# Gated mix of sliding attention and a gated MLP on one core: the last stage's loads, one subtraction, the exponentials and the V weights placed otherwise

## The chip, the cores and the metric

The kernel runs on one core of a Trainium2 chip. The metric is the device time of one execution in microseconds (us). Engines are named as in the profile: PE (matrix), PEld (its weight loads), DVE (vector), ACT (scalar), POOL and SP (here mostly queues that issue DMAs). Each engine works through its own instructions in the order in which the program lists them, and semaphores make it wait for the others.

## The reference

```python
x = A_x                                            # 1 x 2048 x 1024, bf16
g = sigmoid((x * gate_w).sum(-1, keepdims=True))
# A: attention, 32 heads of 32; each position sees itself and 7 earlier ones, 2 apart
q, k, v = heads(x @ wqkv)
logits = einsum("bhsd,bhswd->bhsw", q, k[window]) * 32 ** -0.5   # masked before the start
a = (softmax(logits) weighted sum of v[window]) @ wo
# B: gated MLP, 1024 -> 3584 -> 1024
h = gelu(x @ w_gate) * (x @ w_up)
b = h @ w_down
out = g * a + (1 - g) * b
```

## The kernel before

All matrix products are done by Strassen-like schemes with seven products in place of eight, so DVE has many additions and subtractions of operands and results beside PE's products.

**Units.** The first part is a row of 78 units (0 to 77). Each multiplies 256 weight columns by half of the positions (1024, "s" = 0 or 1): units 0 and 1 are a gate/up pair, 2 to 17 are Q and K, 18 to 25 are V, 26 to 77 are gate (even) and up (odd) units. A unit has seven products, each of four matmuls 128x512 (all at line 362): p1, p5, p26 (two), p73 (two), p4. In step b of the main loop PE gets p1(b), p73(b-1), p5(b), p26(b), p4(b-1), so 28 matmuls. ACT copies a product X to Y's bank after p1 (line 380), puts p5's product aside (385), evacuates X after p26 (368 with Gelu in gate units, 370 otherwise), copies Y to bank Z (392), and evacuates Y after p4. DVE adds p5's part to both Y and Z after p73 (line 399, one instruction for a unit, called "the L399 of unit u" here). p4(u) writes to the bank that the L399 of unit u reads, and ACT's copy to Z (392) of unit u+1 overwrites the other one, so both come after it.

**Background tasks.** All else that DVE does is cut into tasks: generators that issue one instruction or so and yield its estimated cost. `run_bg` is called at the end of each step with a budget of about 4.8 us, and lets the awake task of the lowest priority number go on until the budget is spent. So a task's instructions stand behind the L399 of unit b-1 and ahead of that of unit b. `due` finishes a task at the beginning of a step, `at` puts a call there, `at_end` at the end of one.

Tasks that matter here:
- `qk_prods` (594) and `spill` (594, 645) multiply Q and K; the sums over the head dimension are matmuls (599). The last block of each half is the "spill", done from DRAM copies.
- `softmax` subtracts the maximum (683, 685), `softmax_exp` issues the exponential on ACT (691), which needs another table than Gelu, `softmax_back` sums and normalises (699, 701, 702, 704) and stores the weights.
- `sums_v` (542) makes sums of the V weights, which `load_v` loads; `sums_pair` (319) does so for the gate/up weights.
- `t_forms` (851) makes four combinations of the weights of the last stage (w_down and wo stacked, "R") into DRAM (t_d), with loads at line 837 and three buffers; it stops when V's weights need that memory (`tf_close`, at the end of step TFE-1 = 14), and reloads its buffers when the V units are done.
- `pv_all` multiplies attention weights and V (740, 747) and stores the result o (767).

**Last stage.** `down(s)` multiplies [h, o] by R, once for each half s, with products of 72 matmuls 128x512 (line 1031, `mm`) and, one level further, of 126 matmuls 128x256 (line 1006, `level2`). A quarter Aij has 18 rows of blocks: 0 to 11 and 12, 13 are h, 14 to 17 are o. `mm` takes them in the order 0 to 11, 14 to 17, 12, 13. For s = 0, h must first be multiplied by 1-g (`scale_task`, 895). Then `down(0)` is:

- PE: A11 R11, then A12 R21 on top (both 1031), then `level2` of S and T1, then `level2` of S2 and T2, and so on.
- DVE: scales A12, A22 and A21 (nine instructions, three each), S = A21 + A22 and AD = A11 - A21 (`comb_task`, 902, five instructions each), the forms for S and T1 (967 and 975, eight), S2 = A22 - AD (902), `forms_L` of S2 (967, four), A12 - S2 (902, five), `forms_R` of T2 (975, four).

`level2` begins with two products of plain quarters; the third needs the first results of `forms_L` and `forms_R`. The loads of the first half are issued on SP in this order: A12's h rows, A12's o rows, A22's h, A22's o (all in `pre_down_2`, called at the end of `pv_all`), A21's h, A21's o, then the rows 11 to 17 of R21, from w_down and wo, whose first 11 rows are there earlier (`pre_down_3`, at step 77), then T1 and T2. h loads are line 806, o loads 808, R loads 824, T loads 827. The h rows 12 and 13 are loaded on POOL's queue.

Of the kernel before, what the change touches and what calls it, by code (L numbers as in the profile page):

```python
# [9 lines left out]
ALU = mybir.AluOpType  # L10
# [57 lines left out]
def kernel(  # L68
# [64 lines left out]
    with tc.manual_schedule(engines={mybir.EngineType.PE, mybir.EngineType.DVE, mybir.EngineType.Activation,  # L133
# [296 lines left out]
        def bg(gen, prio, wake):  # L430
            t = Task(gen, prio, wake)
            tasks.append(t)
            tasks.sort(key=lambda t_: t_.prio)
            return t
# [2 lines left out]

        def run_bg(b, period):
            credit[0] = min(credit[0], 0.3) + period
            while credit[0] > 0:  # L440
                t = next((t_ for t_ in tasks if t_.wake <= b), None)
                if t is None:
                    break
                c = t.step()
                if c is None:
                    t.wake = b + 1
                else:
                    credit[0] -= c
# [222 lines left out]
        def softmax(a, cnt, b0, e):  # L671
            ee = regf(R_EX[e], cnt * SC)
            e4 = ee.rearrange("p (a w s) -> p a w s", a=cnt, w=NWIN)
            sw = ee.rearrange("p (a w s) -> p a s w", a=cnt, w=NWIN)
            lg = banks[:, b0:b0 + cnt, :]
            src = lg.rearrange("p a (w s) -> p a w s", w=NWIN)
            bc = lambda t_: t_.rearrange("p a (o s) -> p a o s", o=1).to_broadcast([P, cnt, NWIN, SJ])
            if a == 0:
                TT(out=src[:, 0], in0=src[:, 0], in1=mask, op=ALU.add)
                yield 0.6  # L680
            m = md[:, (0, 2, 0, 3, 0)[e]:(0, 2, 0, 3, 0)[e] + cnt, :]
            assert e < 2 or ready >= {2: {0, 1, 2}, 3: {0, 1, 2}, 4: {4, 5, 6}}[e]
            V.tensor_reduce(out=m, in_=lg.rearrange("p a (w s) -> p a s w", w=NWIN), axis=AX.X, op=ALU.max)
            yield 0.55 * cnt + 0.05
            TT(out=e4, in0=src, in1=bc(m), op=ALU.subtract)
            yield 0.55 * cnt + 0.05
            front.add(a)
            bg(softmax_exp(a, cnt, ee, e4, sw, m, bc), 0, now[0] + 1)

        def softmax_exp(a, cnt, ee, e4, sw, m, bc):  # L690
            nc.scalar.activation(out=ee, in_=ee, func=ACT.Exp, scale=scale)
            bg(softmax_back(a, cnt, ee, e4, sw, m, bc), 3, now[0] + 1)
            yield 0.0

        def softmax_back(a, cnt, ee, e4, sw, m, bc):
            while a // BPS not in gated:
                yield None
            d = m
            V.tensor_reduce(out=d, in_=sw, axis=AX.X, op=ALU.add)
            yield 0.9 * cnt + 0.05  # L700
            V.reciprocal(out=d, in_=d)
            TT(out=d, in0=d, in1=gblk[:, a:a + cnt, :], op=ALU.mult)
            yield 0.65 * cnt
            TT(out=attn_all[:, a:a + cnt, :].rearrange("p a (w s) -> p a w s", w=NWIN), in0=e4, in1=bc(d), op=ALU.mult)
            yield 0.55 * cnt + 0.05
            for j in range(NJ):
                nc.gpsimd.dma_start(out=w_d[a:a + cnt, :, j, :].rearrange("a h n -> h a n"),
                                    in_=attn_all[32 * j:32 * j + 32, a:a + cnt, :])
            ready.update(range(a, a + cnt))
            if a == 2 * BPS - 1:  # L710
                two[0] = True
# [74 lines left out]
        at_slot(Q0 + 6, lambda: gate_chunk(2, bank(1)))  # L786
        at_slot(Q0 + 8, lambda: (gate_chunk(3, bank(1)), bg(gate_task(1), 0, Q0 + 8)))
        due(Q0 + NT + 1, bg(late_form3(), 1, Q0 + 8))
        TFE = Q0 + 13
        due(Q0 + 2 * NT, bg(sums_v(), 2, TFE + 2))  # L790
        for s in range(2):
            for t in range(NT):
# [10 lines left out]

        def load_A(b, s, half, c, i0, i1, with_o, eng=nc.sync):
            t0 = s * SUP + c * SC
            eng.dma_start(out=b[:, i0:i1, :], in_=h_src(half, t0, i0, i1))
            if with_o:
                nc.sync.dma_start(out=b[:, NH_:NK, :], in_=o_d[:, half * 4:half * 4 + 4, t0:t0 + SC])

        def h_src(half, t0, i0, i1):  # L810
            return h_d[:, :, t0:t0 + SC].rearrange("p (i two) s -> p i two s", two=2)[:, i0:i1, half, :]
# [10 lines left out]
        def load_R(b, half, nh, i0=0, i1=NK):  # L822
            for sl, src in r_parts(half, nh, i0, i1):
                nc.sync.dma_start(out=b[:, sl, :], in_=src)
# [8 lines left out]
        def tf_load(q):  # L833
            i0 = NP * q
            for k, a in enumerate(((0, 0), (0, 1), (1, 0), (1, 1))):
                for sl, src in r_parts(*a, i0, i0 + NP):
                    nc.sync.dma_start(out=tf[q % 3][k][:, sl.start - i0:sl.stop - i0, :], in_=src)

        def t_forms():
            q = 0  # L840
            while q < NQ:
                if now[0] == TFE - 1 and tf_open[0]:
                    tf_open[0] = False
                    while now[0] < NQKV + 1:
                        yield None
                    for q_ in range(q, min(q + 3, NQ)):
                        tf_load(q_)
                    yield None
                r11, r12, r21, r22 = tf[q % 3]
                for o_, a, b_ in ((r11, r12, r11), (r12, r22, r12), (r22, r22, r11), (r21, r21, r22)):  # L850
                    TT(out=flat(o_), in0=flat(a), in1=flat(b_), op=ALU.subtract)
                    yield 0.71
                for k, t in enumerate((r11, r22, r12, r21)):
                    nc.gpsimd.dma_start(out=t_d[k][:, NP * q:NP * q + NP, :], in_=t)
                if q + 3 < NQ:
                    tf_load(q + 3)
                q += 1
# [29 lines left out]
        def Bs(s):  # L887
            return {k: bufs[v] for k, v in plan[s].items()}

        def scale_task(b, s, c, ia, ib):  # L890
            t0 = s * SUP + c * SC
            om = omgrep[:, t0:t0 + SC].rearrange("p (o s) -> p o s", o=1)
            for i0 in range(ia, ib, 4):
                i1 = min(i0 + 4, ib)
                TT(out=b[:, i0:i1, :], in0=b[:, i0:i1, :], in1=om.to_broadcast([P, i1 - i0, SC]), op=ALU.mult)
                yield 0.05 + 0.273 * (i1 - i0)

        def comb_task(o_, a, b, op, step=4):
            for i0 in range(0, NK, step):
                i1 = min(NK, i0 + step)  # L900
                f = lambda t_: flat(t_[:, i0:i1, :])
                TT(out=f(o_), in0=f(a), in1=f(b), op=op)  # L902
                yield 0.05 + 0.273 * (i1 - i0)
# [21 lines left out]

        KX = int(R_P5A[0] - R_BUF[6])

        def pre_down_2(s):
            B = Bs(s)
            for k, c in (("A12", 0), ("A22", 1)):  # L930
                load_A(B[k], s, 1, c, 0, NE_, True)
                bg(scale_task(B[k], s, c, 0, NE_), 3, n)

        def pre_down_3(s):
            B = Bs(s)
            load_A(B["A21"], s, 0, 1, 0, NE_, True)
            load_R(B["R21"], 1, 0, KX, NK)

        def pre_down_4(s):
            B = Bs(s)  # L940
# [29 lines left out]
        def forms_R(f, b):  # L970
            f = quads(f)
            q = lambda kh, h: quarter(b, kh, h)
            for o_, a, b_, op in ((f[:, 0], q(0, 1), q(0, 0), ALU.subtract), (f[:, 1], q(1, 1), f[:, 0], ALU.subtract),
                                  (q(0, 1), q(1, 1), q(0, 1), ALU.subtract), (f[:, 2], q(1, 0), f[:, 1], ALU.subtract)):
                TT(out=o_, in0=a, in1=b_, op=op)  # L975
                yield 1.3
# [45 lines left out]
        def down(s):  # L1022
# [53 lines left out]
            run(comb_task(A21, A22, AD, ALU.subtract))  # L1076
            S2 = A21
            level2(VT, S, B["T1"], B["L5"], B["R5"])
            rest = [forms_R(B["R6"], B["T2"]), comb_task(A12, A12, S2, ALU.subtract)]
            run(forms_L(B["L6"], S2), *(rest if last else rest[::-1]))  # L1080

            def mid6():
                joins(VT, B["R5"])
# [58 lines left out]
        for b in range(n):  # L1142
            now[0] = b
            for fn in hooks.pop(b, []):
                fn()
            cur = units[b]
            prv = units[b - 1] if b > 0 else None
            cur.p1()
            if prv:
                prv.p73()  # L1150
            cur.p5()
            extra = 0.0
            if slotq:
                slotq.pop(0)()
                extra += 1.6 if b <= QE + 3 else 0.8
            for fn in pre.pop(b, []):
                fn()
                extra += 0.6
            cur.p26()
            if prv:  # L1160
                prv.p4()
            for fn in post.pop(b, []):
                fn()
            run_bg(b, 4.8 + extra)
# [32 lines left out]
```

## Time and profile before

| | us |
|---|---|
| median of 3 runs | 741.98 (740.92 to 743.15) |
| the profiled execution | 740.5 |
| its span | 738.7 |
| PE busy in the span | 721.3 |
| DVE busy in the span | 654.9 |
| ACT busy | 317.3 |
| mean granted clock of PE | 0.993 |

The span goes from the first to the last instruction; the execution's own time is 1.8 us longer. A line of the waits names the waiting engine and line, what ended the waits, their sum in us, their number and the longest. A line of the timeline has start and length in us, engine, line, operation, output and input, shapes, count, and in brackets the engine's idle time before it and what ended that.

### The profile page before, as it was taken

The page shows a single profiled execution, that of the slowest core. Times are in us where ns is not written, and L with a number is a line of the kernel's source. Part 1 is how long each engine was busy: PE and PEld are TensorE (multiplying, and loading weights), DVE is VectorE, ACT ScalarE, POOL GpSimd, SP SyncE. Part 2 cuts the span into 40 slices and gives each one's busy share as a digit, 9 for nine tenths or more (in the row PEclk, how much of TensorE's full clock was granted, in tenths as well). Part 3 has the DMA queues.
Part 4 walks back from the last instruction along what each step waited for, and adds up shares of the span by engine and source line. Part 5 has one row for each costly group of instructions (what it writes and reads, how often), then busy time and mean ns, then how long its engine had stood idle before and what let it go on. Part 6 is the DMA issues. An engine that isn't in the chain of part 4 may idle for free. (4 is left out here: it accounts for less than half of the span.)

```text
span 738.7 us, 10397 instructions
## 1 busy us (share of the span) xinstructions
PE 721.3 (98%) x3945; PEld 394.5 (53%) x3945; DVE 654.9 (89%) x702; ACT 317.3 (43%) x570; POOL 119.6 (16%) x212
## 2 busy tenths in 40 slices
PE   8999999999999999999999999999989899999998
PEld 4466565655544444444444444444438656758573
DVE  3699999979999999999999999997599699799944
ACT  4554445444566655555555555555102211232210
POOL 1224445311201320000010010101100011110001
PEclk9999999999999999999999999999989999999999
DMA  9977864771326964453364836534982875975501
GB/s 279 272 175 233 277 204 133 256 223 72 107 86 179 362 215 147 118 169 108 123 201 119 269 126 210 168 116 153 356 331 94 333 251 185 367 302 177 216 23 58
DMA packets 118882, 143.93 MB, mean 195 GB/s; under 512 B 18944, under 2 KB 102048, under 8 KB 117808
## 3 DMA queue, kind: packets, MB, share of 16 engines
q1 hardware_dynamic: 104624, 101.53, 43.2%
q0 software_dynamic: 13920, 41.21, 16.5%
q8 instruction: 31, 0.51, 0.3%
q10 hardware_dynamic: 288, 0.52, 0.2%
q14 instruction: 19, 0.16, 0.1%
HBM read 101.16 MB, written 39.99 MB: 191 GB/s over the span
## 5 line engine op out<-in xcount | busy, mean ns | idle before, releaser
L362 PE MATMUL banks<-arena 128*128 128x512 bf16 x2184 | 475.4, 379 | 4.2 <-DVE arena L399 2.4
L362 PEld LDWEIGHTS <-arena 128*128 128x128 bf16 x2184 | 240.5, 111 | 238.5 <-issue 10.5
L1031 PE MATMUL banks<-arena 128*128 128x512 bf16 x504 | 113.1, 386 | 4.6 <-DMA arena<-in_B_w_down_dram 3.1
L399 DVE TENSOR_TENSOR arena<-banks,arena 128x1024 bf16<-128x1024 f32 x78 | 95.2, 1220 | 18.9 <-PE banks L362 11.7
L1006 PE MATMUL banks<-arena 128*128 128x256 bf16 x882 | 99.1, 275 | 3.0 <-DVE arena L975 3.0
L385 ACT COPY arena<-banks 128x512 f32<-128x512 f32 x78 | 45.7, 586 | 130.9 <-PE banks L362 130.9
L1006 PEld LDWEIGHTS <-arena 128*128 128x128 bf16 x882 | 87.1, 99 | 15.3 <-issue 3.5
L1031 PEld LDWEIGHTS <-arena 128*128 128x128 bf16 x504 | 50.0, 99 | 65.7 <-issue 9.2
L370 ACT CAST arena<-banks 128x512 bf16<-128x512 f32 x102 | 59.7, 585 | 43.8 <-PE banks L362 43.8
L740 DVE TENSOR_TENSOR arena<-arena 128x2048 bf16<-128x2048 bf16 x64 | 77.0, 1219 | 0.5
L594 DVE TENSOR_TENSOR arena<-arena 128x2048 bf16<-128x2048 bf16 x64 | 74.8, 1217 | 0.1
L747 DVE TENSOR_TENSOR arena<-arena 128x2048 bf16<-128x2048 bf16 (+2 forms) x96 | 73.7, 775 | 1.0
L256 POOL DMA_DIRECT2D h_d<-arena x28 | 20.0, 716 | 242.9 <-DVE arena L252 204.8
L392 ACT COPY banks<-banks 128x512 f32<-128x512 f32 x78 | 44.5, 571 | 23.4 <-PE banks L362 18.1
L380 ACT COPY banks<-banks 128x512 f32<-128x512 f32 x78 | 45.0, 577 | 13.9 <-PE banks L362 12.8
L1036 POOL DMA_DIRECT2D out_dram<-arena x28 | 15.2, 542 | 183.2 <-DVE arena L1040 128.3
L902 DVE TENSOR_TENSOR arena<-arena 128x2048 bf16<-128x2048 bf16 (+1 forms) x40 | 41.8, 1109 | 0.0
L1011 ACT COPY banks<-banks 128x256 f32<-128x256 f32 x42 | 14.9, 356 | 56.7 <-PE banks L1006 56.5
L319 DVE TENSOR_TENSOR arena<-arena 128x1024 bf16<-128x1024 bf16 x60 | 38.6, 685 | 0.5
L368 ACT ACTIVATE arena<-banks 128x512 bf16<-128x512 f32 x54 | 32.2, 597 | 15.4 <-PE banks L362 15.4
L252 DVE TENSOR_TENSOR arena<-arena 128x2048 bf16<-128x2048 bf16 x28 | 34.0, 1216 | 5.0 <-ACT arena L370 3.7
L967 DVE TENSOR_TENSOR arena<-arena 128x2304 bf16<-128x2304 bf16 x28 | 37.5, 1351 | 0.5
(85 smaller groups left out, 435.6 us busy)
## 6 DMA issues: line engine op xcount, KB each, us to landing
arena<-t_d SPq DMA_DIRECT2D x8, 2304.0 KB, 12.7
h_d<-arena POOLq DMA_DIRECT2D x28, 512.0 KB, 4.1
t_d<-arena POOLq DMA_DIRECT2D x36, 256.0 KB, 4.1
arena<-in_B_w_down_dram SPq DMA_DIRECT2D x5, 1792.0 KB, 12.2
arena<-in_B_w_down_dram SPq DMA_DIRECT2D x32, 256.0 KB, 5.2
arena<-in_B_w_gate_dram SPq DMA_DIRECT2D x15, 512.0 KB, 5.3
arena<-in_B_w_up_dram SPq DMA_DIRECT2D x15, 512.0 KB, 4.5
arena<-h_d SPq DMA_DIRECT2D x4, 1792.0 KB, 11.1
```

What stands on the lines that cost most here:

```text
L362: self.pe = nc.tensor.matmul(ps, lhsT=self.L[form](kt), rhs=rhs[:, kt, :], start=(start and kt == 0), stop=(kt == HK - 1), skip_group_chec ...
L370: nc.scalar.copy(out=o_, in_=i_)
L380: nc.scalar.copy(out=self.Y, in_=self.X)
L385: nc.scalar.copy(out=self.p5s, in_=self.V)
L392: nc.scalar.copy(out=self.Z, in_=self.Y)
L399: TT(out=self.T[:, :, c2s], in0=pair, in1=self.p5s.rearrange("p (o n) -> p o n", o=1).to_broadcast([P, 2, SC]), op=ALU.add)
L594: TT(out=dst, in0=q.rearrange("p (o s) -> p o s", o=1).to_broadcast([P, NWIN, AC]), in1=_win_ap(k, [[-DIL, NWIN], [1, AC]]), op=ALU.mult)
L740: TT(out=prod2[(t // 2) % 2][:, t % 2], in0=ab, in1=_win_ap(v[:, t, HALO:HALO + AC], [[SJ, NJ], [-DIL, NWIN], [1, SJ]]), op=ALU.mult)
L747: TT(out=out_, in0=h(0), in1=h(1), op=ALU.add)
L902: TT(out=f(o_), in0=f(a), in1=f(b), op=op)
L1006: nc.tensor.matmul(c(i, h, j), lhsT=l[:, kt, j * P:(j + 1) * P], rhs=r[:, kt, :], start=False, stop=(kt == KH - 1), skip_group_check=True)
L1031: nc.tensor.matmul(ps, lhsT=L[:, i, j * P:(j + 1) * P], rhs=R[:, i, :], start=(start and q == 0), stop=(q == NK - 1), skip_group_check=not ...
```

## The change

- `run_bg` goes on only while more than 0.3 us of the budget is left, instead of 0.
- The exponential of a softmax is no longer a task; it is put on a list and issued after p26 of the next unit that is not an up unit, so behind ACT's copy to Z. Where it is of a single block, the task that sums it wakes in the same step instead of the next.
- TFE is 14 instead of 15 (`Q0 + 12`), so `tf_close`, `load_v` and `sums_v` come a step sooner. The reload of `t_forms` is put at the beginning of step 27 (NQKV + 1).
- `pre_down_2` loads the h rows of A12 and A22 alone, and A12's scaling wakes a step sooner; `pre_down_3` loads R21's rest, A21's h rows, and then the o rows of A12, A22 and A21.
- For s = 0, A12 - S2 issues three of its five instructions ahead of `forms_R` and two behind it, instead of all five ahead. For s = 1 the order is the same as before.

The computation and the number of instructions on PE, DVE and ACT stay the same. Lines move a little: 691 becomes 693, 699 becomes 700, 701, 702 and 704 become 702, 703 and 705, 740 and 747 become 741 and 748, 806, 808, 824, 827 become 808, 810, 826, 829, 967 and 975 become 975 and 983, 1006 becomes 1014, 1031 becomes 1039.

```diff
         def run_bg(b, period):
             credit[0] = min(credit[0], 0.3) + period
-            while credit[0] > 0:
+            while credit[0] > 0.3:
...
             front.add(a)
-            bg(softmax_exp(a, cnt, ee, e4, sw, m, bc), 0, now[0] + 1)
+            actq.append(lambda: softmax_exp(a, cnt, ee, e4, sw, m, bc))
+
+        actq = []
 
         def softmax_exp(a, cnt, ee, e4, sw, m, bc):
             nc.scalar.activation(out=ee, in_=ee, func=ACT.Exp, scale=scale)
-            bg(softmax_back(a, cnt, ee, e4, sw, m, bc), 3, now[0] + 1)
-            yield 0.0
+            bg(softmax_back(a, cnt, ee, e4, sw, m, bc), 3, now[0] + (0 if cnt == 1 else 1))
...
-        TFE = Q0 + 13
+        TFE = Q0 + 12
...
                 if now[0] == TFE - 1 and tf_open[0]:
                     tf_open[0] = False
-                    while now[0] < NQKV + 1:
+                    at(NQKV + 1, lambda q=q: [tf_load(q_) for q_ in range(q, min(q + 3, NQ))])
+                    while now[0] < NQKV + 2:
                         yield None
-                    for q_ in range(q, min(q + 3, NQ)):
-                        tf_load(q_)
-                    yield None
...
+        def load_h(s, *names):
+            for k in names:
+                load_A(Bs(s)[k], s, int(k[2]) - 1, int(k[1]) - 1, 0, NE_, False)
+
+        def load_o(s, *names):
+            for k in names:
+                load_A(Bs(s)[k], s, int(k[2]) - 1, int(k[1]) - 1, 0, 0, True)
+
         def pre_down_2(s):
-            B = Bs(s)
-            for k, c in (("A12", 0), ("A22", 1)):
-                load_A(B[k], s, 1, c, 0, NE_, True)
-                bg(scale_task(B[k], s, c, 0, NE_), 3, n)
+            load_h(s, "A12", "A22")
+            for k, c, wake in (("A12", 0, n - 1), ("A22", 1, n)):
+                bg(scale_task(Bs(s)[k], s, c, 0, NE_), 3, wake)
 
         def pre_down_3(s):
             B = Bs(s)
-            load_A(B["A21"], s, 0, 1, 0, NE_, True)
             load_R(B["R21"], 1, 0, KX, NK)
+            load_h(s, "A21")
+            load_o(s, "A12", "A22", "A21")
...
-            rest = [forms_R(B["R6"], B["T2"]), comb_task(A12, A12, S2, ALU.subtract)]
-            run(forms_L(B["L6"], S2), *(rest if last else rest[::-1]))
+            run(forms_L(B["L6"], S2))
+            rest = comb_task(A12, A12, S2, ALU.subtract)
+            if not last:
+                take(rest, 3)
+            run(forms_R(B["R6"], B["T2"]), rest)
...
             cur.p26()
+            while actq and cur.kind != "up":
+                actq.pop(0)()
             if prv:
                 prv.p4()
```

## The prediction

> **What bounds the kernel now.** I read the page's busy times, then the waits of the matrix engine, then the timeline around each wait.
>
> ```profile
> PE 721.3 (98%) x3945; PEld 394.5 (53%) x3945; DVE 654.9 (89%) x702; ACT 317.3 (43%) x570; POOL 119.6 (16%) x212
> ```
> ```profile
> PE banks L1031 <- DMA arena<-in_B_w_down_dram: 3.1, 1, 3.1
> PE banks L1006 <- DVE arena L975: 3.0, 1, 3.0
> PE banks L362 <- DVE arena L399: 2.4, 4, 0.9
> PE banks L362 <- ACT banks L380: 1.3, 2, 0.7
> ...
> PE banks L1031 <- DMA arena<-in_A_wo_dram: 1.1, 1, 1.1
> ```
>
> The matrix engine (PE) is the bound: 17 us idle in all, so time can only come out of waits. In the list, 7.2 us stand in the last stage (lines 1031, 1006) and 3.7 us in the unit stage (line 362). An idle stretch costs twice, as the windows (length, PE, PEld, DVE, ACT, POOL, granted clock, DMA) show:
>
> ```profile
> 535.00:538.30 3.30, 0.18 (x1) 0.10 (x1) 2.83 (x3) 0.00 (x0) 0.00 (x0) 1.00 1.16 373
> 538.40:545.20 6.80, 5.70 (x15) 1.97 (x14) 6.80 (x8) 0.58 (x1) 0.57 (x1) 0.52 1.01 421
> ...
> 575.90:579.30 3.40, 2.84 (x14) 2.04 (x14) 3.29 (x4) 0.37 (x1) 0.00 (x0) 0.54 1.02 434
> 579.40:587.00 7.60, 7.60 (x70) 6.79 (x69) 2.92 (x4) 3.77 (x9) 0.00 (x0) 0.99 0.71 250
> ```
>
> After the idle 3.14 us (and 1.10 more) the clock stood near half for 6.8 us, after the idle 3.05 us for 3.4 us: about 3.4 and 1.4 us more lost (the second counted from PE's restart at 576.46).
>
> In the unit stage DVE has hardly any room either. Its L399 of unit u starts after p73(u) (0.09 us later at best), takes 1.22, and must end before p4(u), for which PE gets ready 2.59 us after p73's end (counted off the trace's single matmuls, 28 of line 362 to a step): room of about 1.25 us, more where a reduction by matmuls stands in the step. What DVE has queued between two L399 is thus paid by PE as soon as it overruns by 1.25 us.
>
> **Exponentials and their reduces: the dearest part.** The exponentials of the two spilled blocks run now between unit steps, and DVE's sum over them (L699) comes late enough never to wait:
>
> ```profile
> 215.51 0.57 ACT L392 COPY banks<-banks 128x512 f32<-128x512 f32 x1 [0.27 <-PE banks L362]
> ...
> 216.98 1.28 ACT L691 ACT_TABLE_LOAD   x1
> 218.21 1.22 DVE L594 TENSOR_TENSOR arena<-arena 128x2048 bf16<-128x2048 bf16 x1
> 218.27 0.63 ACT L691 ACTIVATE arena<-arena 128x512 f32<-128x512 f32 x1
> ...
> 219.34 1.22 DVE L399 TENSOR_TENSOR arena<-banks,arena 128x1024 bf16<-128x1024 f32 x1
> ...
> 224.14 1.04 DVE L699 TENSOR_REDUCE md<-arena 128x64 f32<-128x512 f32 x1
> ```
>
> In the changed order the exponential stands behind Z's copy (L392) of unit 28, and, since a single block's sum now wakes in the same step with priority over the spill's products, the sum stands directly behind the L399 of unit 27, ahead of two products. The second pair is the same: exponential behind the copy of unit 34, sum behind the L399 of unit 33, ahead of four L851. Count from the end of p73(27), 212.88: the copy of unit 28 ends 3.20 us later (216.08), the table load and the exponential end at 3.2 + 1.28 + 0.65 = 5.1. DVE has ended its L399 at about 2.4 and idles some 2.7 us. Queued behind the waiting sum are, on DVE, the sum and its three followers (2.4 us from start to start: 224.14 to 225.10, then 226.23 to 227.68), two products (2.27) and then the L399 of unit 28, for which PE waits. It starts at 5.2 + 2.4 + 2.3 = 9.9 and ends at 11.1; PE is ready for p4(28) at 6.05 + 2.59 = 8.6. PE waits **2.5 us**. In step 34 the same count has four L851 (2.8 us, 254.81 to 257.59) instead of two products and 2.5 for the sum's group: 11.7 against 8.6, **3.1 us**. The gain of the same edit: the first exponentials (2.96 us of ACT at 115.9) move ahead of one evacuation, which saves at most 0.3 of the 0.69 at 119.46; the 0.60 at 251.86 goes.
>
> **The budget threshold and the V weights.** No instruction is added; tasks slip by a step. V's four sums (4.8 us) go from ahead of the L399 of unit 17 to ahead of unit 16's: the 0.87 wait at 149.51 goes. Their weights must then be there at about 135 (the L399 of unit 15 ends at 134.75); now they are issued at 128.39 and land at 139.92. One step earlier (their SP queue is behind four small loads that wait for stores of the L851 pair, which also move up a unit) gives an issue near 122 and a landing near 133.5: just in time. Were they to land as now, DVE would idle 4.7 us and PE some 2. Unit 22 loses one product (1.13 us), so its wait of 0.85 goes. On the other side the L851 pair moved into unit 13 adds 1.39 us there (PE waits 0.95 in place of 0.69), and one more L851 in unit 10, whose L399 ends 0.19 us ahead of the deadline now, costs 0.55. Twelve loads of the reload (L837) move ahead of two pair loads on SP: their buffers come free at 203.3, 3.1 MB at the 336 GB/s seen there need to 213, while the next pair load waits for its buffer to 210.3 and 216.4 and is used at 221.6: hidden, and DVE's 1.3 us of idling for them and PE's 0.45 at 246.79 go. The wait of 0.27 at 177.24 stays. POOL's stores of t and of the weights move with their tasks by a step; nobody waits for them within one. That an edit does not reach the program is no case: the built order of instructions has each of them.
>
> Sum of the unit stage, waits now: 0.69 + 0.87 + 0.27 + 0.85 + 0.45 + 0.60 = 3.7. Then: 0.55 + 0.95 + 0.27 + 2.5 + 3.1 = 7.4. **+3.7 us.** Whether gaps of 2.5 and 3.1 us drop the clock depends on how they lie: the row of 3.05 had 2.5 us of it before the change of clock at 575.9 and lost 1.4 behind it; gaps under 0.9 lost nothing. One of the two doing so, **+1.7** (half of 3.4), is the likeliest; bounds 0 and 5.
>
> **Loads of the first half.** PE's 3.14 + 1.10 us wait for R21's last rows, which lie last in SP's queue; in the new order they go ahead of A21, and A12's o part goes behind it. By bytes from SP's release at 515.0 (the last o store landing, for which A22's load then waits instead of A12's o): A21's rows have 0.13 MB less ahead of them, at 350 GB/s 0.4 us, and land at 535.1 instead of 535.44; A12's o at 536.6, PE reaches those rows at 534.97 + 12 x 0.213 = 537.5. So the 4.2 us and the 3.4 us behind them all go. But DVE works from A21's landing without a gap:
>
> ```profile
> 535.47 3.50 DVE L895 TENSOR_TENSOR arena<-arena,omgrep 128x2048 bf16<-128x2048 bf16 x3 [5.00 <-DMA arena<-h_d]
> ```
> ```profile
> 569.92 5.22 DVE L902 TENSOR_TENSOR arena<-arena 128x2048 bf16<-128x2048 bf16 x5
> ...
> 575.06 5.35 DVE L975 TENSOR_TENSOR arena<-arena 128x2304 bf16<-128x2304 bf16 x4
> 576.46 11.49 PE L1006 MATMUL banks<-arena 128*128 128x256 bf16 x90 [3.05 <-DVE arena L975]
> ```
>
> PE's earlier arrival is spent there. **A12 - S2 in two parts** takes two of the five L902 (1.13 + 0.63 = 1.75 us) from ahead of the first L975; with the 0.4 it ends at 574.25 and PE restarts at 574.3, after 6.0 us idle (it arrives at 568.3 = 534.97 + 15.45 for 72 matmuls + 17.9). It starts 2.15 us sooner. The slow stretches of the windows were one and two times 3.4 us: one where the first of them held 0.54 us of idling, two where it held 1.10. After 6.0 us the restart falls anywhere in such a stretch, so 2.8 to 6.3 us at half clock follow it instead of 2.9: 2.3 lost instead of 1.4. **-1.25 us** (bounds -2.2 and 0). The two deferred L902 end by 580, before joins' turn and long before A12's next use at 587. A12's scaling, moved ahead of unit 77's L399, delays it to 519.4; p4(77) is at 519.49: free, by 0.1.
>
> Sum against the profiled execution: 740.5 + 3.7 + 1.7 - 1.25 = 744.6. The median of the runs lies 1.5 above it: **746.1**.
>
> **Rivals.**
> - The sums find their exponentials ready: DVE idles under the 1.25 us of room at units 28 and 34. For it: L699 never waited so far. Against it: 1.9 us of ACT work start behind a copy that itself follows the L399 in front of the sum. It decides if the exponential ends by 3.7 us after p73 instead of 5.1. Then 5.6 and 1.7 go: 746.1 - 7.3 = 738.8, faster. Chance 0.11.
> - The clock holds in both gaps: 744.4, right at the edge of what can be told from no change. The trace speaks against it with 3.05 us. Chance 0.16. [...]
> - V's weights land no sooner: 2 us more, 748.1. Chance 0.08.
> - DVE is not the bound of the last stage, so its waits and half clock (7.65 + 4.49) go whole: 746.1 - 12.1 + 1.25 = 735.3. For it only that these are the longest waits; against it the unbroken DVE chain. Chance 0.05.
>
> **How the numbers follow.** The forecast holds 0.60. Range 742.0 (no half clock, the last stage's full gain, less offset to the median) to 749.5 (two windows at half, nothing from the last stage): left out are the two faster rivals, 0.16, and a little. What a measurement can tell from no change is 0.3%, 2.2 us. Slower: 0.58 of the forecast, 0.08, half of 0.16: 0.74. Same 0.10, faster 0.16.
>
> **What would show it.** PE waits of 2 to 3.5 us on L399 in steps 29 and 35, DVE idle some 2.7 us before the sum (L700 then) with ACT as its releaser; no wait on w_down or A_wo in the last stage, and some 6 us on the first forms_R instead. Wrong if L700 does not wait, or the matmuls behind forms_R restart more than 3 us sooner than now.

## The result and the profile after

| | before | after |
|---|---|---|
| median, side by side on one chip | 742.22 (740.92 to 743.15) | 747.01 (746.73 to 747.17) |
| profiled execution, its span | 740.5, 738.7 | 747.2, 745.4 |
| mean granted clock of PE | 0.993 | 0.991 |

Times in us. The ratio is 1.0065, 95% interval 1.0048 to 1.0083: slower by some 4.8 us. The page and the waits of the matrix engine in the changed kernel:

```profile
PE 722.1 (97%) x3945; PEld 394.8 (53%) x3945; DVE 655.0 (88%) x702; ACT 317.6 (43%) x570; POOL 120.1 (16%) x212
```
```profile
PE banks L362 <- DVE arena L399: 8.1, 6, 3.1
PE banks L1014 <- DVE arena L983: 6.8, 1, 6.8
PE banks L1039 <- DMA arena<-o_d: 1.8, 1, 1.8
```

The work is the same; the waits lie elsewhere. Those for w_down and A_wo are gone, the one at the first `forms_R` (now L983) grew from 3.05 to 6.76, and the L399 waits from 2.4 to 8.1 us. The timeline around unit 28 tells where the last come from:

```profile
216.23 1.28 ACT L693 ACT_TABLE_LOAD   x1
217.52 0.63 ACT L693 ACTIVATE arena<-arena 128x512 f32<-128x512 f32 x1
218.19 1.04 DVE L700 TENSOR_REDUCE md<-arena 128x64 f32<-128x512 f32 x1 [2.94 <-ACT arena L693]
...
222.98 1.22 DVE L399 TENSOR_TENSOR arena<-banks,arena 128x1024 bf16<-128x1024 f32 x1
...
224.25 5.95 PE L362 MATMUL banks<-arena 128*128 128x512 bf16 x19 [2.61 <-DVE arena L399]
```

DVE, which has no time to spare here, stands idle 2.94 us for the exponential; the sum's group, two products and then L399 follow, and PE gets the bill: 2.61 us. At unit 34 it is 3.57 us of DVE idle and 3.11 us of PE. The windows show what came behind the two gaps (columns: length, PE, PEld, DVE, ACT, POOL, granted clock, DMA share, GB/s; the cuts are those of the clock's changes):

```profile
221.49:224.90 3.41, 0.80 (x5) 0.29 (x3) 3.41 (x4) 0.59 (x2) 1.60 (x4) 1.00 0.15 39
224.90:228.31 3.41, 3.41 (x10) 1.21 (x9) 3.38 (x6) 3.29 (x4) 0.74 (x1) 0.50 0.30 79
262.45:265.86 3.41, 0.56 (x3) 0.17 (x2) 3.31 (x5) 0.32 (x1) 3.41 (x7) 1.00 0.23 73
265.86:269.27 3.41, 3.15 (x8) 1.16 (x8) 3.41 (x4) 3.08 (x4) 2.51 (x5) 0.50 0.85 314
```

Both gaps were followed by 3.41 us at half clock, in which PE worked 3.41 and 3.15 us. Its 128x512 matmuls started 0.427 us apart there, against 0.216 behind the first of them at full clock, so half of that, 3.3 us, is lost besides. In the last stage PE's first wait there is a new one, and DVE's chain ends in the `forms_R` gap:

```profile
543.45 3.50 DVE L895 TENSOR_TENSOR arena<-arena,omgrep 128x2048 bf16<-128x2048 bf16 x3 [7.95 <-DMA arena<-h_d]
...
544.98 13.12 PE L1039 MATMUL banks<-arena 128*128 128x512 bf16 x60 [1.75 <-DMA arena<-o_d]
...
581.30 5.35 DVE L983 TENSOR_TENSOR arena<-arena 128x2304 bf16<-128x2304 bf16 x4
582.70 7.57 PE L1014 MATMUL banks<-arena 128*128 128x256 bf16 x50 [6.76 <-DVE arena L983]
```

**The account.** Line 362's waits in units 10 to 34 sum to 8.24 us where they were 3.73: +4.5; half clock +3.3; so A11 R11 starts 8.0 us later (524.07 for 516.04, 0.2 of it small change). Counted from that start, `forms_R` lets PE go on 1.79 us sooner, and the `level2` behind it ends 1.35 us sooner. 8.0 - 1.35 = 6.7 us, which is what the two profiled executions differ by (747.2 - 740.5). The medians differ by 4.8 only: the profiled execution of before was shorter than the four it was measured with, that of after the longest of its four.

### The profile page after: what moved, and what is told of

Same layout as the page of the kernel before. It is cut to its first block, busy times and chain, and to the rows that moved or that the text cites. A ratio compares the mean times of both kernels' runs of the same rounds, so it can differ in the third digit from the quotient of the medians.

```text
span 745.4 us, 10405 instructions
## 1 busy us (share of the span) xinstructions
PE 722.1 (97%) x3945; PEld 394.8 (53%) x3945; DVE 655.0 (88%) x702; ACT 317.6 (43%) x570; POOL 120.1 (16%) x212
## 5 line engine op out<-in xcount | busy, mean ns | idle before, releaser
L399 DVE TENSOR_TENSOR arena<-banks,arena 128x1024 bf16<-128x1024 f32 x78 | 95.2, 1220 | 19.3 <-PE banks L362 9.3
L741 DVE TENSOR_TENSOR arena<-arena 128x2048 bf16<-128x2048 bf16 x64 | 77.0, 1219 | 0.4
L594 DVE TENSOR_TENSOR arena<-arena 128x2048 bf16<-128x2048 bf16 x64 | 74.6, 1218 | 0.1
L975 DVE TENSOR_TENSOR arena<-arena 128x2304 bf16<-128x2304 bf16 x28 | 37.5, 1351 | 0.5
L983 DVE TENSOR_TENSOR arena<-arena 128x2304 bf16<-128x2304 bf16 x28 | 37.5, 1351 | 0.2
```

The source lines that it names most:

```text
L399: TT(out=self.T[:, :, c2s], in0=pair, in1=self.p5s.rearrange("p (o n) -> p o n", o=1).to_broadcast([P, 2, SC]), op=ALU.add)
L594: TT(out=dst, in0=q.rearrange("p (o s) -> p o s", o=1).to_broadcast([P, NWIN, AC]), in1=_win_ap(k, [[-DIL, NWIN], [1, AC]]), op=ALU.mult)
L741: TT(out=prod2[(t // 2) % 2][:, t % 2], in0=ab, in1=_win_ap(v[:, t, HALO:HALO + AC], [[SJ, NJ], [-DIL, NWIN], [1, SJ]]), op=ALU.mult)
```

## The experiments

The kernel before ran again beside each, with medians of 741.6 to 742.1; ratios are to it. Their edits shift lines a little: the last stage's `forms_R` is L975, 976, 983 or 984, its matmuls L1006, 1007, 1014 or 1015.

**The exponentials alone.** The kernel before with this one edit:

```diff
-            bg(softmax_exp(a, cnt, ee, e4, sw, m, bc), 0, now[0] + 1)
+            actq.append(lambda: softmax_exp(a, cnt, ee, e4, sw, m, bc))
...
-            bg(softmax_back(a, cnt, ee, e4, sw, m, bc), 3, now[0] + 1)
-            yield 0.0
+            bg(softmax_back(a, cnt, ee, e4, sw, m, bc), 3, now[0] + (0 if cnt == 1 else 1))
...
+            while actq and cur.kind != "up":
+                actq.pop(0)()
```

> The kernel before with the edit of the exponentials alone (behind the copy to Z, sum of a single block in the same step). Theory: two waits of PE of 2.5 to 3.5 us at units 28 and 34 with up to 3.4 us lost at half clock, less the 0.6 of the removed wait on L380: 747 to 751 us against 742.2. Rival: within 1 us of the kernel before.

Measured 748.1, ratio 1.0097 (1.0083 to 1.0112): this edit alone costs 6.4 us, more than the whole change. PE waited 2.60 and 2.39 us, and only behind the second did the clock fall:

```profile
219.98:223.39 3.41, 1.47 (x7) 0.58 (x6) 3.41 (x4) 0.96 (x2) 2.00 (x4) 1.00 0.11 29
223.39:226.81 3.42, 2.75 (x13) 1.26 (x13) 3.38 (x5) 2.69 (x4) 0.74 (x1) 1.00 0.15 41
260.94:264.35 3.41, 1.02 (x6) 0.39 (x5) 3.34 (x6) 0.60 (x2) 2.00 (x4) 1.00 1.10 362
264.35:267.77 3.42, 3.42 (x9) 1.23 (x9) 3.42 (x4) 3.38 (x4) 2.10 (x4) 0.50 0.35 126
```

In the traces of before and after the times at which the clock changes lie 3.41 us or whole multiples of it apart (the times stand in the last section); such a row of points is called the grid here, and a stretch between two neighbouring points a cell. The longer gap was split by a grid point, 1.94 us on one side and 0.66 on the other, and no half clock followed; the shorter one lay inside one cell, and a cell at 0.50 followed. That is taken up below.

**The sum a step later.** The changed kernel with one line altered:

```diff
-            bg(softmax_back(a, cnt, ee, e4, sw, m, bc), 3, now[0] + (0 if cnt == 1 else 1))
+            bg(softmax_back(a, cnt, ee, e4, sw, m, bc), 3, now[0] + 1)
```

> The changed kernel with one thing undone: the sum over a single block's exponentials wakes a step later again, so it stands behind the L399 of units 28 and 34 instead of 27 and 33. Theory (the sum waits on DVE for an exponential that stands behind a copy of the same step): the two waits of 2.61 and 3.11 us and the 3.15 us lost at half clock behind them go, 747.0 - 8.9 = 738.1 us (737 to 739.5). Rival (the loss comes from the budget threshold and the new places of the exponentials on ACT, not from the sum): 745 to 747.

Measured 739.24, ratio 0.9967 (0.9956 to 0.9978). The waits at units 28 and 34 and their half clock are gone, 7.8 us by the medians and 7.3 by the ratios: the waiting sum is shown to be the cause, and not the exponential's place on ACT, which stayed. The median is 1.1 above the middle of what was expected. In the profiled execution, the longest of the eleven (741.42), V's weights landed later (139.42, issued at 124.83) and DVE waited for them; whether they did so in the others is not shown:

```profile
139.55 4.88 DVE L542 TENSOR_TENSOR arena<-arena 128x2048 bf16<-128x2048 bf16 x4 [3.05 <-DMA arena<-in_A_wqkv_dram]
```

PE paid 1.15 and 1.74 us at units 16 and 17.

**V weights as before.** The last kernel with TFE back at 15:

```diff
-        TFE = Q0 + 12
+        TFE = Q0 + 13
```

> The changed kernel with the sum a step later again and, besides, the V weights at their place before (TFE = Q0 + 13). Theory (a step sooner is too soon for their load: DVE idled 0.9 to 3.0 us for them and PE then 0.9 to 2.9 at units 16 and 17): 1 to 2 us less than with the sum alone put back, 737.2 to 738.2 us. Rival (the waits at units 16 and 17 come from the six products queued there, not from the load): 739 to 740.

Measured 738.47, ratio 0.9957 (0.9945 to 0.9969), between the two expectations. DVE idled 0.35 in place of 3.05 us for the weights; PE waited 0.49 us at unit 15, behind six products of DVE, and 0.95 at unit 17, behind V's sums. The interval overlaps that of the kernel with the weights sooner: what the earlier weights cost is within a us or so, and no gain shows.

**The budget's end.** The kernel with the sum a step later, with `while credit[0] > 0:` as before, weights still sooner:

> The changed kernel with the sum a step later (as in the first experiment, 739.24 there against 741.69) and the budget's end at 0 again, V weights still issued a step sooner. V's four sums then stand a step later again, behind the sum of a softmax, and the weights (139.4 in the first experiment) should be there or nearly. Theory (PE's 1.15 and 1.74 us at units 16 and 17 come from DVE idling 3.05 us for weights that the budget's end asks for a step too early): both shrink to under 0.9 us together, unit 10's 0.59 goes, units 13 and 22 have about 0.69 and 0.3 to 0.85 as in the kernel before; PE's waits of line 362 fall from 5.1 to 2.5-3.5 us, time 737.2 us (736.3 to 738.3). Rival (the weights land no sooner whatever stands ahead, and DVE idles as much): 739.2 us, DVE idle at least 2 us ahead of the first L542.

Measured 740.09, ratio 0.9986 (0.9974 to 0.9998): the rival's side, 0.9 above its figure. The edit did not do what was expected of it. V's sums stand ahead of the L399 of unit 16 in both kernels; only one product moved from ahead of them to behind them. So DVE was ready for them at 134.66 in place of 136.50 and idled 2.42 us, although the weights landed at 136.96 and not at 139.42. PE's reduction by matmuls (L599), behind DVE's late product, waited 2.50 us for it:

```profile
137.08 4.88 DVE L542 TENSOR_TENSOR arena<-arena 128x2048 bf16<-128x2048 bf16 x4 [2.42 <-DMA arena<-in_A_wqkv_dram]
```

In both traces the sums start as the transfer lands, so the transfer sets this wait; a later place of the sums with the weights a step sooner is not tested by this run. Why issues at 123.5 to 124.8 landed at 136.5 to 139.4 stays open.

**The last stage alone** (loads and the split of A12 - S2, on the kernel before), and its two halves each by itself:

> The kernel before with the two edits of the last stage alone (load order, A12 - S2 in two parts). Theory (DVE's chain from A21's landing sets when PE goes on): PE restarts at forms_R about 1.8 us sooner and loses about 0.5 more at half clock, so 740.9 us (739.8 to 741.9) against 742.2, although the waits on w_down and wo of 4.2 us and 3.4 us of half clock are gone. Rival (the loads were the bound): those 7.6 us go whole, 734.6.

> The kernel before with the load order of the first half alone. Theory (DVE's chain from A21's landing sets when PE goes on): the waits on w_down and wo and the half clock behind them (7.6 us) go, but PE waits some 8.5 us at forms_R, which it leaves at most 0.4 sooner, and loses some 1 to 2 us more at half clock behind so long a gap: 742.3 us (740.8 to 743.5) against 741.7. Rival (the loads were the bound): 734.

> The kernel before with A12 - S2 in two parts alone. Theory: forms_R starts 1.75 us sooner, the wait of 3.05 at it shrinks to some 1.3, too short for the half clock, so the 1.4 us behind it go as well: 741.7 - 3.2 = 738.5 us (737.5 to 740), faster than both last-stage edits together (739.5), since the waits on the loads were paid ahead of a chain that PE has to wait for anyway. Rival (the two edits work only together): 741 to 742.

Measured 739.53, ratio 0.9974 (0.9966 to 0.9983), for both; 741.67, ratio 1.0000 (0.9991 to 1.0009), for the loads alone; 738.54, ratio 0.9966 (0.9952 to 0.9980), for the split alone. The first lies 0.3 below its range: PE went on 1.7 us sooner than in the kernel before (1.8 expected), but the 0.5 more at half clock did not come. The loads give nothing that can be told, as DVE's chain takes PE's earlier arrival back: its wait at `forms_R` became

```profile
PE banks L1015 <- DVE arena L984: 8.5, 1, 8.5
```

with 10.24 us at half clock behind it, 6.0 of which PE worked through. All the gain of this part is in the split, which takes 1.75 us out of that chain. In the split alone PE kept its 2.99 + 1.11 us of waits for rows. Its gap at `forms_R` was 2.49 us and not the 1.3 expected, as only one cell at half clock followed those waits and PE came 1.3 us sooner; in the profiled execution the clock stayed at 1.00 behind it:

```profile
570.54:573.95 3.41, 1.55 (x15) 1.24 (x13) 3.41 (x4) 0.00 (x0) 0.00 (x0) 1.00 1.18 388
573.95:577.37 3.42, 2.79 (x26) 2.51 (x26) 3.32 (x4) 0.74 (x2) 0.00 (x0) 1.00 1.01 431
```

It is split by a grid point, as the first gap of the exponentials alone. The runs of this kernel lie between 737.3 and 742.2 us, and their mean clocks go with that: the eight of 737.3 to 738.6 us had 0.995 to 0.998, the four of 740.0 to 742.2 us 0.993. That these gaps fell otherwise to the grid there fits, but no trace of those four shows it.

**A21's h rows ahead of A22's.** If the chain from A21's landing is the bound, that landing is what to move. The edit is on top of the kernel with both last-stage edits; A21's rows then go ahead of R21's rest too:

```diff
         def pre_down_2(s):
-            load_h(s, "A12", "A22")
-            for k, c, wake in (("A12", 0, n - 1), ("A22", 1, n)):
-                bg(scale_task(Bs(s)[k], s, c, 0, NE_), 3, wake)
+            load_h(s, "A12")
+            bg(scale_task(Bs(s)["A12"], s, 0, 0, NE_), 3, n - 1)
 
         def pre_down_3(s):
             B = Bs(s)
+            load_h(s, "A21", "A22")
+            bg(scale_task(B["A22"], s, 1, 0, NE_), 3, n)
             load_R(B["R21"], 1, 0, KX, NK)
-            load_h(s, "A21")
             load_o(s, "A12", "A22", "A21")
```

> As the kernel with the two last-stage edits alone, but A21's h rows are loaded ahead of A22's instead of behind R21: they need not wait for the last o store, so DVE scales A21 by about 530.5 instead of 539, and S can begin then. Theory (DVE's chain is the bound): the wait of PE at forms_R of some 6.8 us shrinks by 4 us or goes, and the half clock with it, 733 to 737 us. Rival (the amount of data on the queue is the bound, its order not): as with the two edits alone, 740 to 742.

Measured 733.44, ratio 0.9895 (0.9880 to 0.9911), against 0.9974 without this edit. A21's h rows landed at 519.77 instead of 535.51, DVE's longest idle stretch in the stage fell from 7.74 us to 1.86, and the `forms_R` gap from 6.76 to 3.25 us:

```profile
569.54 12.81 PE L1015 MATMUL banks<-arena 128*128 128x256 bf16 x90 [3.25 <-DVE arena L984]
```

**All of A12 - S2 behind `forms_R`** (the last kernel without `take(rest, 3)`):

> The last-stage edits with A21 loaded ahead of A22, and all five instructions of A12 - S2 behind forms_R. Theory (the three left ahead of it are all that PE still waits for): forms_R starts 3.4 us sooner, the remaining wait of 3.25 us goes and with it the 3.4 us lost at half clock, 733.4 - 6.6 = 726.8 us (726 to 729). Rival (something else is late next, T1's reads that forms_R has to wait for, or A12 - S2 now too late for its use): 730 to 734.

Measured 729.36, ratio 0.9831 (0.9817 to 0.9844); a mean clock of 1.000. The gap is 0.32 us:

```profile
566.60 9.66 PE L1015 MATMUL banks<-arena 128*128 128x256 bf16 x87 [0.32 <-DVE arena L984]
```

It came out 0.4 above the expected 726 to 729: 4.1 us less than the last kernel by medians, 5.2 between the profiled executions (734.99 and 729.75), where 2.9 of the gap and 2.9 of half clock (5.83 us at half, from 569.54 to 575.37) went and 0.6 came back elsewhere.

**The parts that help, together**: the changed kernel with the sum a step later, V weights as before, A21 first and all of A12 - S2 behind `forms_R`; and the same with the budget's end at 0.

> The changed kernel with what helped: sum a step later, V weights as in the kernel before, A21's h rows ahead of A22's, and all of A12 - S2 behind forms_R. Theory (the parts lie in different stages and add): the unit stage of the experiment with V weights as before (738.47, PE waits of line 362 some 2.9 us in place of 4.0 where the unit stage is that of before) and the last stage of the experiment with forms_R first (729.36): 729.4 - 1.1 = 728.3 us (727.3 to 729.3), PE's gap at the first forms_R under 0.6 us, unbroken clock. Rival (a PE that comes sooner to the last stage only waits there for loads that are tied to the last stores): 729.4 us or more, with PE waits on A21's or A12's rows of over 1 us in the last stage.

> As the other kernel of this call, with the budget's end at 0 as in the kernel before, so that of the exponentials' edit only the place on ACT is left and nothing of the task order by the budget. Theory (the budget's end moves waits between units and hardly changes their sum): PE waits of line 362 between 2.5 and 4.0 us, time 728.8 us (727.5 to 730). Rival (the budget's end of 0.3 is what saves the 0.87 and 0.85 us of units 17 and 22 and the 0.45 later): 730 to 731 us, with those waits back.

Measured 727.3, ratio 0.9809 (0.9795 to 0.9822), and 728.2, ratio 0.9817 (0.9804 to 0.9831): the stages' gains add, and the budget's end makes no difference that can be told. The first is 14.8 us faster than the kernel before and 19.7 faster than the changed one by medians. From its page and waits:

```profile
PE 712.7 (98%) x3883; PEld 392.8 (54%) x3945; DVE 654.4 (90%) x702; ACT 317.6 (44%) x570; POOL 120.1 (17%) x212
```
```profile
PE banks L362 <- DVE arena L399: 2.1, 5, 0.6
```

The mean granted clock is 1.000. Its PE busy time of 712.7 us can't be set against the 721.3 of before, as 62 of the 3945 matmuls are missing from the trace; in the kernel with `forms_R` first, where none is missing and the mean clock is 1.000 too, PE was busy for 716.6 us, 4.7 less than before with the same matmuls.

## Why the prediction was right

The forecast 746.1 and its range held the 747.01, and the mechanism was the predicted one, but for V's weights and A12's o rows, which it had too early. By its steps:

- **The two sums.** 2.5 and 3.1 us were predicted, 2.61 and 3.11 measured, with DVE idle 2.94 us ahead of the first (some 2.7 predicted). The rival that finds the exponentials ready fell.
- **Half clock in the unit stage.** +1.7 was taken for one gap of the two; in the profiled execution 3.41 us at half clock followed each: 3.3. This term was mis-sized most. The working said that it depends on how the gaps lie, but had no rule for that; by the estimate below, one gap of the two had a chance of 0.49 and both 0.36, so which it was is luck. The other three executions had mean clocks of 0.992 and 0.993 for 0.991, so less of them was at half clock; where, no trace shows. The rival that the clock holds in both fell: half clock followed gaps of 2.61 and 3.11 us here, and one of 2.39 with the exponentials alone.
- **V weights.** An issue near 122 and a landing near 133.5 were predicted, "just in time"; they were issued at 124.00 and landed at 136.52, and DVE idled 0.89 us:

```profile
136.65 4.88 DVE L542 TENSOR_TENSOR arena<-arena 128x2048 bf16<-128x2048 bf16 x4 [0.89 <-DMA arena<-in_A_wqkv_dram]
```

  The chain from there to the L399 of unit 17 has no gap, so PE's wait there stayed (0.89, was 0.87). SP's small loads ahead of the weights were issued up to 123.50, later than the working had it, and from issue to landing it took 12.5 us instead of 11.5. This is the larger part of the difference between 8.24 and the predicted 7.4 us of waits.
- **Units 10, 13, 21, 22, 32.** 0.55, 0.95, 0.27, 0 and 0 predicted; 0.59, 0.78 (0.15 + 0.63), 0.26, 0 and 0 measured.
- **A12's o rows.** "No wait" was wrong: PE waited 1.75 us. The 12 matmuls were added to 534.97, a time that already stood behind 11 of them; PE was there at 535.2 on the clock of before (544.98 - 1.75 - 8.03). It cost nothing, since PE's arrival is spent at `forms_R` anyway.
- **The last stage.** -1.25 predicted, -1.35 measured from the stage's start; PE's restart 2.15 sooner predicted, 1.79 measured: A21's rows came 20.2 us after SP's release instead of 20.4 (0.4 predicted, 0.2 got), and the release itself lay 0.2 later in the stage. Behind the restart 4.0 us stood at half clock, so 2.0 were lost, where 2.3 were taken. The loads alone at 1.0000 and the split alone at 0.9966 show the claim that DVE bounds this stage, and the rival with all waits gone (735.3) fell.
- **The sum.** Unit stage +3.7 predicted, +4.5 measured; half clock +1.7 for +3.3; last stage right. Together 2.5 us more than forecast between profiled executions. Since the offset of 1.5 from the profiled execution to the median did not show in the changed kernel (747.2 profiled, 747.0 median), the miss in the median is only 0.9: two errors of opposite sign, and that part of the agreement is luck. The offset goes with half clock as well: of 60 executions of the kernel before beside the experiments, the 25 with a mean clock of 0.990 have a median of 742.1 us, the 12 with 0.995 one of 740.8; the profiled one had 0.993.
- **Slips that changed little.** The 6.8 us at half clock behind the first waits held 5.70 us of PE's work, so 2.9 us were lost there and not 3.4, and the second stretch went on to 579.58, which makes 1.6 of the 1.4; the -1.25 uses the second of them, the rival of 735.3 both. The range's upper end comes to 749.1 by its own terms, not 749.5.

## What to carry to other kernels

Where an engine has about a microsecond of room in each step, ask of a moved task not when its input is issued but when it is ready, and what queues behind the wait: the sum itself costs the same in either step, only its early place cost 7 to 8 us. A shorter wait of the bounding engine is worth nothing while another engine's chain ends later; find the first landing from which that chain has no gap, and move that landing or take work off the chain. And look at the clock behind a PE gap as well: here gaps of 2.39, 2.61, 3.05 and 3.11 us were each followed by 3.41 us at half clock, 1.6 to 1.7 us more lost, and one of 3.25 by 6.83 us, 2.9 more, while two of 2.49 and 2.60 us were followed by none.

## What the runs showed of the hardware

The clock changed at 538.62, 545.45, 576.17 and 579.58 us in the profiled execution of before, and at 224.90, 228.31, 265.86, 269.27, 579.89 and 586.71 in that of after: 3.41 us apart or whole multiples of it. To the span's start the grid lay otherwise in each (first point at 2.73 us before, 3.03 after, 1.93 in the kernel with A21 first, 0.52 in the split alone). I cut along it before and after from end to end, and in five experiments (the exponentials, the loads and the split alone, A21 first, the budget's end) the stretches around gaps. In these cells PE's idle time went with the clock of the next one. A cell at full clock with 2.25 us of PE idle or more (nine cells; the rows below show the least, in the kernel with A21 first) was each time followed by half clock; none with 1.94 or less was. Of the cells at half clock, those with 0.29 us idle or less were followed by full clock, and those with 0.82 or more by half again.

```profile
565.13:568.54 3.41, 1.16 (x11) 0.88 (x10) 3.41 (x4) 0.00 (x0) 0.00 (x0) 1.00 1.21 419
568.54:571.96 3.42, 2.42 (x12) 1.69 (x12) 3.31 (x3) 0.26 (x1) 0.00 (x0) 0.50 1.01 431
571.96:575.37 3.41, 3.41 (x18) 2.34 (x17) 3.41 (x5) 0.49 (x2) 0.00 (x0) 0.50 0.24 97
```

Here a cell with 3.41 - 1.16 = 2.25 us idle was followed by half clock, and the next one, with 1.00 us idle, by another at half. The five executions of this kernel go with it: the one with a mean clock of 1.000 took 731.81 us, the four with 0.995 to 0.998 took 733.3 to 735.0. So in these runs the price of a gap went with its place on the grid, and not with its length alone (2.39 us inside a cell, 2.60 us split as 1.94 and 0.66). With a limit near 2.1 us (between 1.94 and 2.25), an estimate from these numbers is that a gap of length g, laid at random, is followed by half clock in (3.41 + g - 2 x 2.1) / 3.41 of the cases: 0.53 for 2.6 us, 0.68 for 3.1. The limits are read from these runs alone, and no run was made to place a gap at will.
